# A GpSimd memset moved ahead of the first weight loads, and one W1 piece moved into an earlier group of tiled matmuls

## The chip, the cores and the metric

The kernel runs on one core of a Trainium2 chip. The metric is the device time of one execution in microseconds (us). Every execution also has a span, from the first to the last instruction in the trace; the span is about 1.8 us under the time. One core has no second die to compare with, so "fast" in the run lists means only that an execution is within 1.5% of the fastest of its kernel.

## The reference, cut to what matters

```python
def _attn_ref(x, state):              # x: (8, 8, 512, 64), state: (8, 8, 32, 64)
    a = softmax(scale * x @ state^T)
    xread = a @ state
    a2 = softmax(scale * state @ x^T)
    sread = a2 @ x
    return concatenate([xread, sread], axis=2)

def _moe_ref(x, w_in, w_out):         # w_in: (512, 2048), w_out: (2048, 512)
    h = x @ w_in
    return (h * sigmoid(h)) @ w_out
```

The attention output, 8 x 544 rows of 512, goes through the two-layer network. The kernel doesn't form `xread`. It folds the state into the weights: for each batch b it computes W(b) = state(b) @ w_in, called W0 and W1 for batches 0 and 1, and then h = a @ W(b). W has 2048 columns and is computed in pieces of up to 512.

## The kernel before

Each piece of W is eight small matmuls, placed on 64 x 32 tiles of the array:

```python
def w1_mms(b, cols, new=bank):
    ...
    for f, n in cols:
        for hg in range(2):
            pss[f, hg] = new([128, 512], FP32, "ps_w1")
        for s in range(4):
            for hg in range(2):
                ...
                nc.tensor.matmul(pss[f, hg][ds(32 * s, 32), 0:n],
                                 stT[ds(r, 64), b, h // 2, s % 2, :],
                                 w_in_sb[ds(r, 64), h // 2, ds(f, n)],
                                 ..., tile_position=(r, 32 * s))
```

The matmuls write into buffers called PSUM banks. `bank` hands out the banks a2 and a3 in turn; `new_h` hands out the two buffers h1. The first batch runs through 12 steps. `upto` issues first-layer products (g1, the matmuls called h), `G2` second-layer products (called o, or o_a for two of the row blocks):

```python
W0 = {2: (512, 512), 6: (1024, 512), 10: (1536, 512)}
W1_AT = {4: 0, 6: 512}
LEAD0 = [2, 2, 2, 2, 2, 3, 2, 1, 3, 3, 2, 3]
T3 = {1: (0, 1), 2: (2,), 3: (3,), 4: (4,), 5: (5,), 6: (6,)}
for ft in range(12):
    upto(min(ft + LEAD0[ft], ready))
    if ft == 1:
        place_one_state(1, transpose_one_state(st1_n), nc.vector)
    if ft in W0:
        pss = w1_mms(0, [W0[ft]])
        if ft in W1_AT:
            pss1 = w1_mms(1, [(W1_AT[ft], 512)], new_h)
        w1_out(0, [W0[ft]], both, pss)
        ...
    elif ft in W1_AT:
        w1_cols(1, [(W1_AT[ft], 512)], both)
    ...
    for tt in range(3):
        G2(0, tt, ft)
    for i in T3.get(ft, ()):
        G2(0, 3, i)
```

The loads at the start: x of batch 0 in two halves on the sync queue, the weights from GpSimd behind a small identity matrix. GpSimd later casts a quarter of the second half of x.

```python
make_identity(nc, ident)            # GpSimd
load_w_in(0, 128); load_w_in(128, 384)
load_w_out(0, 2); load_w_out(2, 2)
...                                 # state of batch 1
load_w_in(512); load_w_out(4, 4)
...
cast_x(0, nc.gpsimd, 0, 1, 4, 4)    # a quarter of the second half of x
...
for i in range(3):                  # at 21.6 us
    ones_beside_x(i, nc.gpsimd)     # two memsets each
```

The softmax here doesn't subtract the row's maximum and nothing guards it: scores larger than these inputs give would overflow.

## Time and profile before

| | before |
|---|---|
| median of 4 executions | 212.99 us (212.90 to 213.12) |
| the profiled execution | 214.55 us, span 212.8 |
| TensorE busy | 97% of the span |
| first second-layer matmul (o) | 13.84 us |

In the lines of the profile, PE is TensorE's matmul, PEld its weight load, DVE VectorE, ACT ScalarE, POOL GpSimd and SP the sync queue; L468 is line 468 of the kernel.

How to read it: TensorE is the bound, so a gain has to come from TensorE's list of work or from the 13 us before that list runs without holes. The profiled execution is over 1.4 us slower than each of the four timed ones.

### The profile page before, as it was taken

The page shows a single profiled execution, that of the slowest core. Times are in us where ns is not written, and L with a number is a line of the kernel's source. Part 1 is how long each engine was busy: PE and PEld are TensorE (multiplying, and loading weights), DVE is VectorE, ACT ScalarE, POOL GpSimd, SP SyncE. Part 2 cuts the span into 40 slices and gives each one's busy share as a digit, 9 for nine tenths or more (in the row PEclk, how much of TensorE's full clock was granted, in tenths as well). Part 3 has the DMA queues.
Part 4 walks back from the last instruction along what each step waited for, and adds up shares of the span by engine and source line. Part 5 has one row for each costly group of instructions (what it writes and reads, how often), then busy time and mean ns, then how long its engine had stood idle before and what let it go on. Part 6 is the DMA issues. An engine that isn't in the chain of part 4 may idle for free.

```text
span 212.8 us, 3839 instructions
## 1 busy us (share of the span) xinstructions
PE 205.8 (97%) x1550; PEld 97.9 (46%) x1575; DVE 73.8 (35%) x146; ACT 139.1 (65%) x244; POOL 39.9 (19%) x62
## 2 busy tenths in 40 slices
PE   7899999999999999999999999999999999999993
PEld 2543445345444434444444444444444444466653
DVE  2672246855851137104410752143512306100011
ACT  2685667899676877699469856886775256644410
POOL 8393213702420122012200302000200000000000
PEclk9999999999999999999999999999999999999998
DMA  5999999995639567464826429114230121011112
GB/s 189 192 205 207 285 261 313 249 242 203 99 78 265 174 130 170 101 195 102 218 64 211 79 53 240 49 52 99 65 83 17 64 82 52 0 49 49 52 49 99
DMA packets 42929, 28.65 MB, mean 135 GB/s; under 512 B 28064, under 2 KB 37792, under 8 KB 42912
## 3 DMA queue, kind: packets, MB, share of 16 engines
q1 hardware_dynamic: 36720, 20.65, 36.3%
q0 software_dynamic: 5904, 7.64, 17.4%
q8 instruction: 12, 0.20, 0.4%
q10 hardware_dynamic: 288, 0.13, 0.2%
q14 instruction: 5, 0.04, 0.1%
HBM read 17.43 MB, written 8.91 MB: 124 GB/s over the span
## 4 chain that ended last, share of the span: by engine, by line
PE 94%; DMA 2%; DVE 1%; issue 1%; ACT 0%
PE o L563 50%; PE h L522 26%; PE ps_w L468 4%; PE h L543 3%; PE o_a L563 3%; DMA x_f<-in_x_dram 2%; PE o_part L585 2%; PE ps_xt L252 1%; PE ps_sr L415 1%; PE ps_busy L165 1%; PE ps_sc L305 1%; PE ps_scT L331 1%; DVE W L159 1%; PE ps_at L397 0%; ACT xT L157 0%
## 5 line engine op out<-in xcount | busy, mean ns | idle before, releaser
L563 PE MATMUL o<-w_out_sb,g 128*128 128x512 bf16 x481 | 129.5, 379 | 1.3 <-issue 0.5
L554 ACT ACTIVATE g<-h 128x512 bf16<-128x512 f32 (+1 forms) x143 | 81.3, 573 | 35.3 <-PE h L522 20.6
L563 PEld LDWEIGHTS <-g 128*128 128x128 bf16 x528 | 50.2, 98 | 58.9 <-issue 3.8
L522 PE MATMUL h<-aT,W 128*128 128x512 bf16 x247 | 73.1, 379 | 0.2
L159 DVE COPY o_sb<-o 128x512 f32<-128x512 f32 x15 | 10.4, 690 | 91.9 <-PE o L563 87.3
L522 PEld LDWEIGHTS <-W 128*128 128x128 bf16 x254 | 24.4, 98 | 30.7 <-issue 1.2
L159 DVE CAST W<-ps_w 128x512 bf16<-128x512 f32 (+2 forms) x36 | 22.3, 658 | 23.8 <-PE ps_w L468 23.8
L157 ACT ACTIVATE W<-ps_w 128x512 bf16<-128x512 f32 (+1 forms) x32 | 16.3, 562 | 10.2 <-PE ps_w L468 10.2
L159 POOL CAST x_nat<-x_f 128x512 bf16<-128x512 f32 x24 | 14.6, 648 | 33.2 <-DMA x_f<-in_x_dram 33.2
L157 ACT ACTIVATE o_sb<-o 128x512 f32<-128x512 f32 x16 | 9.5, 597 | 14.3 <-PE o L563 11.8
L361 POOL TENSOR_TENSOR an<-e,rcn 128x512 bf16<-128x512 bf16 x5 | 7.6, 1517 | 49.1 <-DVE rcn L359 49.1
L468 PE MATMUL ps_w<-w_in_sb,stT 64*32 64x512 bf16 (+2 forms) x264 | 10.2, 374 | 0.0
L543 PE MATMUL h<-xmT,w_in_sb 128*128 128x256 bf16 x64 | 9.6, 273 | 0.1
L563 PE MATMUL o_a<-w_out_sb,g 128*128 128x512 bf16 x30 | 9.4, 379 | 0.1
L543 PEld LDWEIGHTS <-w_in_sb 128*128 128x128 bf16 x64 | 6.3, 98 | 3.9
L165 PE MATMUL ps_busy<-busy 128*128 128x512 bf16 x15 | 6.8, 563 | 1.2 <-DVE warm L172 1.2
L358 DVE TENSOR_REDUCE rs<-e 128x32 f32<-128x1024 bf16 x5 | 6.1, 1210 | 2.1 <-DMA e<-eT 2.1
L345 ACT ACTIVATE eT<-ps_scT 128x512 bf16<-128x512 f32 x10 | 5.4, 594 | 1.6 <-PE ps_scT L331 1.6
L784 ACT ACT_TABLE_LOAD x5 | 6.4, 1283 | 0.1
L381 POOL TENSOR_TENSOR an<-exp_nat,rc 128x512 bf16<-128x512 bf16 x3 | 3.1, 1046 | 17.7 <-ACT eT L345 10.8
L468 PEld LDWEIGHTS <-stT 64*32 64x32 bf16 x264 | 3.2, 90 | 5.5 <-issue 4.7
L109 POOL DMA_DIRECT2D x_f<-in_x_dram x4 | 3.3, 845 | 10.2 <-DVE x_rows L159 7.9
(76 smaller groups left out, 103.7 us busy)
## 6 DMA issues: line engine op xcount, KB each, us to landing
out_dram<-o_sb SPq DMA_DIRECT2D x33, 256.0 KB, 2.4
x_f<-in_x_dram SPq DMA_DIRECT2D x4, 1024.0 KB, 5.8
x_f<-in_x_dram POOLq DMA_DIRECT2D x2, 1024.0 KB, 11.1
w_in_sb<-in_moe_w_in_dram POOLq DMA_DIRECT2D x3, 512.0 KB, 10.1
x_f<-in_x_dram SPq DMA_DIRECT2D x2, 512.0 KB, 5.2
w_out_sb<-in_moe_w_out_dram POOLq DMA_DIRECT2D x4, 256.0 KB, 11.4
w_out_sb<-in_moe_w_out_dram POOLq DMA_DIRECT2D x2, 512.0 KB, 11.2
x_f<-in_x_dram POOLq DMA_DIRECT2D x2, 512.0 KB, 13.5
```

Source lines behind the costliest of these rows:

```text
L157: nc.scalar.activation(dst, src, func=COPY, bias=0.0)
L159: eng.tensor_copy(dst, src)
L165: nc.tensor.matmul(ps[:], busy[:, 0:128], busy[:], start=True, stop=True, skip_group_check=True)
L345: nc.scalar.activation(t[:, hg], scT_ps[hg][:], func=EXP, bias=0.0, scale=SCALE)
L358: nc.vector.tensor_reduce(rs[:], e2[b][:], axis=AX, op=ADD)
L361: eng.tensor_tensor(a[:, hg], e2[b][:, hg], rc[:, hg].to_broadcast([128, 4, 4, NS]), op=MULT)
L468: nc.tensor.matmul(pss[f, hg][ds(32 * s, 32), 0:n], stT[ds(r, 64), b, h // 2, s % 2, :], w_in_sb[ds(r, 64), h // 2, ds(f, n)], start=True, ...
L522: nc.tensor.matmul(h_ps[k][:], W1[b][:, hg, ds(128 * ft, 128)], aT[b][:, hg, :, :], start=(hg == 0), stop=(hg == 1), skip_group_check=True,)
L543: nc.tensor.matmul(ps[:, 0:256], w_in_sb[:, kt, ds(128 * ft, 128)], xmT[:, :, kt].rearrange("p t n b -> p t (n b)"), start=(kt == 0), stop ...
L554: nc.scalar.activation(g[:, 0:n], ps[:, 0:n], func=SILU, bias=0.0)
L563: nc.tensor.matmul(outs[tt][:], gt[b * NFT + ft][:, ds(128 * tt, 128)], w_out_sb[:, ft, :], start=(ft == 0), stop=(ft == NFT - 1), skip_gr ...
L784: nc.scalar.activation(warm[:], busy[:, 0:1], func=SILU, bias=0.0)
```

## The change

Its intent: GpSimd spends a memset before it starts the weight loads, so that they begin half a microsecond later and leave the DMA engines to x. And the W1 piece of step 4 joins the W0 piece of step 2, so that the tiled mode is entered once for both. The rest of the diff makes room: h products 4 and 5 take the banks of the W pieces, because the W1 piece holds both h1 buffers, and product 3 comes a step earlier.

```diff
     make_identity(nc, ident)
+    ones_beside_x(0, nc.gpsimd)
     load_w_in(0, 128)
@@ g1_half
-            pool, tag = (psA, "a1") if k == 1 else (psH, "h1")
-            h_ps[k] = pool.tile([128, 512], FP32, tag=tag, name="h1")
+            if k == 1:
+                h_ps[k] = psA.tile([128, 512], FP32, tag="a1", name="h1")
+            else:
+                h_ps[k] = (bank if k in IN_BANKS else new_h)([128, 512], FP32, "h1")
@@
+    IN_BANKS = (4, 5)
@@
-    for i in range(3):
+    for i in (1, 2):
         ones_beside_x(i, nc.gpsimd)
@@
-    W1_AT = {4: 0, 6: 512}
-    LEAD0 = [2, 2, 2, 2, 2, 3, 2, 1, 3, 3, 2, 3]
+    W1_AT = {2: 0, 6: 512}
+    LEAD0 = [2, 3, 2, 2, 2, 3, 2, 1, 3, 3, 2, 3]
@@
-        elif ft in W1_AT:
-            w1_cols(1, [(W1_AT[ft], 512)], both)
```

## The prediction

> **What bounds the kernel now.** I read the head of the page first, then the chain of waits in order of time, then the timeline of the first 24 us, the only stretch that the change touches.
>
> ```profile
> PE 205.8 (97%) x1550; PEld 97.9 (46%) x1575; DVE 73.8 (35%) x146; ACT 139.1 (65%) x244; POOL 39.9 (19%) x62
> PE 94%; DMA 2%; DVE 1%; issue 1%; ACT 0%
> ```
>
> TensorE is busy 97% of the span and holds 94% of the chain that ends last. The other 2% is one wait, at the very start:
>
> ```profile
> 0.74 4.74 DMA x_f<-in_x_dram
> 5.51 0.57 DVE x_rows L159
> 6.12 1.03 PE ps_xt L252 x8
> ...
> 16.65 0.41 PE ps_w L468 x8
> 17.07 0.69 DVE W L159
> 17.80 0.60 PE h L522 x2
> ```
>
> The first half of x (512 KB) lands at 5.48 us and everything up to the first real matmul hangs on it through casts, transposes and softmax. From 13.4 us on, TensorE issues a 512-column matmul every 0.216 us with almost no hole. So two kinds of gain are open: x landing sooner (shifts everything), or fewer microseconds of TensorE after 13.4 us. The places where it loses pace near the change are the tiled W matmuls (ps_w):
>
> ```profile
> 16.06 0.59 PE L522 MATMUL h<-aT,W 128*128 128x512 bf16 x2
> 16.58 0.41 PE L468 MATMUL ps_w<-w_in_sb,stT 64*32 64x512 bf16 x8
> 16.92 0.61 PE L563 MATMUL o<-w_out_sb,g 128*128 128x512 bf16 x2
> ...
> 19.64 0.41 PE L468 MATMUL ps_w<-w_in_sb,stT 64*32 64x512 bf16 x8
> 19.98 0.61 PE L563 MATMUL o<-w_out_sb,g 128*128 128x512 bf16 x2
> 20.42 0.59 PE L563 MATMUL o_a<-w_out_sb,g 128*128 128x512 bf16 x2
> 20.85 1.03 PE L522 MATMUL h<-aT,W 128*128 128x512 bf16 x4
> 21.71 0.59 PE L563 MATMUL o<-w_out_sb,g 128*128 128x512 bf16 x2
> 22.14 0.59 PE L563 MATMUL o_a<-w_out_sb,g 128*128 128x512 bf16 x2
> 22.67 0.63 PE L468 MATMUL ps_w<-w_in_sb,stT 64*32 64x512 bf16 x16
> 23.23 0.60 PE L563 MATMUL o<-w_out_sb,g 128*128 128x512 bf16 x2
> ```
>
> Read starts, not durations: durations include the drain of the pipeline. The two h at 16.06 occupy 2 x 0.216 and should end at 16.49; the o after the group of eight starts at 16.92, so that group costs 0.43 us. The group of sixteen: the second o_a of 22.14 ends its turn at 22.58, the next o starts at 23.23: 0.65 us. Two groups apart cost 2 x 0.435 = 0.87, two groups together 0.65. (Where fewer records than the program has matmuls stand between two starts, as after 16.92, a record is missing; the starts show the slot.)
>
> **What the Trainium skill says.** (1) "TensorEngine Tiling (Array Packing)", section Key Properties: changing the tiling mode drains TensorE. The trace agrees: 0.09 us from 16.49 to 16.58 on entry and about 0.1 us on leaving, for each group of 64*32 between 128*128 matmuls, whatever its length. (2) "DMA: Bandwidth & Descriptors", section Issuing engines are not separate DMA queues: DMAs from any engine run on the same 16 DMA engines and interleave. This is the case for delaying the weights: leave the engines to x. The trace shows little of it to gain (below). (3) Same page, section SWDGE vs HWDGE vs iDMA: for a DMA issued from GpSimd a core of it computes the descriptors, so a memset ahead of the load delays the load. The trace agrees: the GpSimd issues stand one after another at 0.71 to 0.93 us each from 1.44 to 6.56 us.
>
> **Part 1, the memset ahead of the weights.** It moves one pair of GpSimd memsets (0.33 and 0.13 us, starts 0.29 us apart from pair to pair) from 21.6 us to 1.3 us. All GpSimd issues after it move 0.3 to 0.5 us later: the pair unpipelined is 0.33 + 0.13 = 0.46 us.
>
> ```profile
> 1.44 1.68 POOL L150 DMA_DIRECT2D w_in_sb<-in_moe_w_in_dram  x2
> 3.10 1.42 POOL L153 DMA_DIRECT2D w_out_sb<-in_moe_w_out_dram  x2
> 5.02 0.79 POOL L150 DMA_DIRECT2D w_in_sb<-in_moe_w_in_dram  x1
> 7.00 0.40 POOL L159 CAST x_rows<-x_f 128x256 bf16<-128x256 f32 x1 [0.44 <-DMA x_f<-in_x_dram]
> ```
>
> Gain: does x land sooner? In the packet records by queue, x has its queue to itself until 4.96 us; the first weight packet starts there, just when the DMA engines finish their shares of x one by one (4.99 to 5.08 on six, 5.6 to 5.95 on nine, 6.44 on the last). The half that the chain waits for has its last packet done at 4.96. The second half takes 1.42 us on most engines and the first half about the same (32 packets of 46 ns are 1.47), so the weights don't slow it either. Expected gain: 0. Whether the weights then start later at all is open: they were issued at 1.44 and started 3.5 us later, apparently behind x, so half a microsecond of later issue may be hidden.
>
> Cost: landing times from each issue against the first use (issue start + landing): w_in columns 0 to 127 land at 1.44 + 6.0 = 7.4, used 10.32; the next 384 at 2.2 + 7.5 = 9.7, used 11.25; w_out 0, 1 at 3.1 + 8.0 = 11.1, used 13.84; w_in 512 to 1023 at 5.02 + 10.1 = 15.1, used 16.58. The least room is 1.5 us, over the 0.5 lost. The GpSimd cast at 7.00 waited for x until 6.97; GpSimd comes free at 6.56 + 0.46 = 7.02 instead, so it slips by under 0.1 us, and its transposes start at 8.29, behind a warm-up matmul. Cost: 0. The later loads (from 11.42) start behind a softmax product on GpSimd and are not moved by it.
>
> **Part 2, the W1 piece.** Removed: the lone group of eight at 19.64. Added: the same eight behind the eight of 16.58. Matmuls and copies stay the same in number; one entry and one exit of the tiled mode go. On TensorE: 0.87 - 0.65 = 0.22 us. The starts give slightly more: from 16.49 to 20.85 there are sixteen matmuls of 0.216 (3.45 us) and two groups, so 0.91 for the groups with the slow first matmuls behind them; from 22.58 to 24.10 there are four (0.86) and one double group, 0.66. 0.91 - 0.66 = **0.25 us**, all on the path.
>
> Moved: the first-layer product k=3 comes one step earlier (LEAD0 2 to 3), since the W1 group takes both h1 buffers in step 2; k=4 and 5 go to the banks of the W group. I count the new order from 14.49: four h (0.86), the state transpose at 15.35, five second-layer matmuls to 16.49, sixteen tiled ones to 17.14, four to 18.00, then k=4. Its waits: the W0 copies, DVE 17.05 to 17.74 and ACT 17.18 to 17.77, are done before 18.00 (before, k=4 came at 17.80, right on the DVE copy); the W1 copies follow to 18.4 on DVE and 18.3 on ACT, and ACT is then free for the silu of k=4 (18.6). The h1 buffers are wanted again by k=6 at 20.6, long free. The W1 group needs the state of batch 1:
>
> ```profile
> 15.18 0.96 DVE L159 COPY stT<-ps_st 64x64 bf16<-64x64 bf16 x4 [1.18 <-PE ps_st L206]
> ```
>
> Its transpose moves 0.43 us back, behind the h of k=3, so these copies end at 16.14 + 0.43 = 16.57, and the second group's matmuls are due at about 16.81, with weight loads of 0.09 before them. It fits with 0.1 to 0.2 us over: the tightest place of the change. Later stages move 0.25 us forward as one piece: w_in 1024 lands at 11.42 + 8.8 = 20.2 for a use at 22.4, w_in 1536 at 25.4 for a use at 27.6, x of batch 1 at 28.3 for its second cast at about 29.3.
>
> **The sum.** 212.99 - 0 - 0.25 = 212.74, rounded to 212.7 us.
>
> **Rivals.** (a) *x lands sooner.* For it: all loads share engines, and nine of them begin x 0.7 us later than the first six, for a reason that I don't see. If GpSimd's descriptor work at 1.4 to 2.3 us has a part in that, the delay brings some of it to the front: 0.2 to 0.5 us more, 212.2 to 212.5. Against it: no weight packet moves before 4.96. (b) *The state copies come too late.* TensorE would stand in the double group for 0.1 to 0.3 us and eat the gain: 212.8 to 213.0. Against it: the count above, though by little. (c) *Weights become the wait.* If the delay grew in the queue to over 1 us, w_in 512 would arrive after its use at 16.5 and push everything: 213.2 or more. Against it: the room of 1.5 us, and an unbroken stream of packets that a later issue doesn't interrupt. (d) *The gain is given back* at a later wait for DMA (x of batch 1) or DVE: 213.0. Against it: TensorE has the chain from 13 us to the end.
>
> **Range and chances.** The three runs before spread 0.22 us, so the median itself is good to about 0.1. With (a) below and (b), (c), (d) above, 212.3 to 213.0. Two per cent is 4.3 us; nothing here reaches that. Faster 0.01, same 0.98, slower 0.01.
>
> **What would show it.** Part 1: the first weight load issued near 1.9 us, x still landing at 5.5 (half a microsecond sooner would prove rival (a)), no wait for a weight. Part 2: sixteen ps_w in one piece near 16.6, none near 19.6, the o after them 0.65 us after the last matmul before them, k=4 at about 18.0 with no wait, and k=6 at 20.6 instead of 20.85. From there all starts should be 0.25 us earlier to the end. Wrong if PE waits for DVE stT in the double group, if W copies hold k=4, or if the shift is lost by 52 us.

## The result

The changed kernel took 212.86 us (median of 4, 212.69 to 213.12) against 212.99 us. The ratio is 0.9995, with a 95% interval from 0.9977 to 1.0012: the same within 2%, as predicted, and too small to be seen in so few executions. (A ratio is the mean time of one kernel's fast runs over that of the other's of the same rounds, so not quite the ratio of the medians quoted.)

The page of the changed kernel, the two lines that answer to those shown of before:

```profile
PE 205.3 (97%) x1575; PEld 96.8 (46%) x1575; DVE 74.0 (35%) x146; ACT 139.2 (66%) x244; POOL 39.5 (19%) x62
PE 95%; DMA 2%; DVE 1%; ACT 0%; issue 0%; DVEq 0%
```

Nothing has moved in the bound. The span, though, is 210.9 us against 212.8, which is 1.9 us, where the timed executions differ by 0.13 us. Its chain of waits (start, duration, what) begins:

```profile
0.74 4.17 DMA x_f<-in_x_dram
5.01 0.44 DVE x_rows L159
```

x landed at 4.91 us instead of 5.48, which at first looks like rival (a) of the prediction. The timeline of TensorE shows a second difference. These are the same eight transposes of x, before and then changed:

```profile
6.12 1.03 PE L252 MATMUL ps_xt<-ident,x_rows 128*128 128x128 bf16 x8 [0.44 <-DVE x_rows L159]
```

```profile
5.50 0.62 PE L253 MATMUL ps_xt<-ident,x_rows 128*128 128x128 bf16 x8 [0.54 <-DVE x_rows L159]
```

1.03 us against 0.62 for equal work: TensorE was still slow in the trace of before. Warm-up matmuls (on zeros, to keep TensorE busy) stand 0.43 us apart in both traces until 3.7 us, and 0.22 us apart from 4.4 us on in the changed one. The clock records of the traces say when full speed was granted: at 10.2 us in the trace of before, at 3.9 us in the changed one. The Trainium skill, "TensorE: Matmul & The Clock Gate", section Part 1: The HAM clock gate, says that the window which watches activity runs free, so the number of slow matmuls at the start varies from run to run. The traces here agree: the same kernel before was at full speed from 10.2 us in its first trace, and from 6.9 and 5.1 us in e1 and e12 below. The two late ones of the 14 (10.2 us, and 10.6 in e4) are also the two in which the first half of x landed last, at 5.48 and 5.34 us; in the other twelve it landed at 4.79 to 5.11 us, and full speed came at 3.9 to 6.9 us. So the 1.9 us is no effect of the change, and the stage of the tiled matmuls must be read by itself.

The timeline of TensorE, changed kernel (start, duration, engine, line, operation):

```profile
13.80 0.59 PE L566 MATMUL o<-w_out_sb,g 128*128 128x512 bf16 x2
14.23 0.81 PE L566 MATMUL o_a<-w_out_sb,g 128*128 128x512 bf16 x3
14.99 0.64 PE L469 MATMUL ps_w<-w_in_sb,stT 64*32 64x512 bf16 x16
15.56 0.60 PE L566 MATMUL o<-w_out_sb,g 128*128 128x512 bf16 x2
...
19.03 1.03 PE L525 MATMUL h<-aT,W 128*128 128x512 bf16 x4
...
20.85 0.63 PE L469 MATMUL ps_w<-w_in_sb,stT 64*32 64x512 bf16 x16
```

The sixteen stand together and no group stands near 18. GpSimd's timeline has the surprise of part 1:

```profile
1.25 0.31 POOL L115 MEMSET x_rows<- 128x256 bf16 x1
...
1.50 0.11 POOL L118 MEMSET x_rows<- 128x16 bf16 x1
1.55 1.68 POOL L150 DMA_DIRECT2D w_in_sb<-in_moe_w_in_dram  x2
```

The first load is issued at 1.55 us, and before at 1.44. The memset delays the weights by 0.11 us, not by half a microsecond. Its pair takes 0.36 us, from 1.25 to 1.61 us. Of that, 0.06 us run beside the last step of the identity matrix (which ends at 1.31), 0.13 us fill the gap that stood ahead of the load before, and 0.06 us run beside the load; 0.11 us are left.

### The profile page after: what moved, and what is told of

Its sections match the earlier page's. It is cut to its first block, busy times and chain, and to the rows that moved or that the text cites. A ratio compares the mean times of both kernels' runs of the same rounds, so it can differ in the third digit from the quotient of the medians.

```text
span 210.9 us, 3866 instructions
## 1 busy us (share of the span) xinstructions
PE 205.3 (97%) x1575; PEld 96.8 (46%) x1575; DVE 74.0 (35%) x146; ACT 139.2 (66%) x244; POOL 39.5 (19%) x62
## 4 chain that ended last, share of the span: by engine, by line
PE 95%; DMA 2%; DVE 1%; ACT 0%; issue 0%; DVEq 0%
PE o L566 51%; PE h L525 26%; PE ps_w L469 4%; PE h L546 3%; PE o_a L566 3%; DMA x_f<-in_x_dram 2%; PE o_part L588 2%; PE ps_sr L416 1%; PE ps_xt L253 1%; PE ps_sc L306 1%; PE ps_scT L332 1%; PE ps_busy L165 1%; PE ps_at L398 0%; PE h L507 0%; DVE W L159 0%; ACT xT L157 0%
## 5 line engine op out<-in xcount | busy, mean ns | idle before, releaser
L566 PE MATMUL o<-w_out_sb,g 128*128 128x512 bf16 x496 | 131.8, 379 | 0.0
L525 PE MATMUL h<-aT,W 128*128 128x512 bf16 x254 | 74.5, 379 | 0.1
L566 PE MATMUL o_a<-w_out_sb,g 128*128 128x512 bf16 x32 | 10.0, 379 | 0.0
L165 PE MATMUL ps_busy<-busy 128*128 128x512 bf16 x16 | 5.8, 481 | 1.2 <-DVE warm L172 1.2
## 6 DMA issues: line engine op xcount, KB each, us to landing
w_in_sb<-in_moe_w_in_dram POOLq DMA_DIRECT2D x3, 512.0 KB, 10.2
```

The lines of the kernel that those rows point to most:

```text
L165: nc.tensor.matmul(ps[:], busy[:, 0:128], busy[:], start=True, stop=True, skip_group_check=True)
L525: nc.tensor.matmul(h_ps[k][:], W1[b][:, hg, ds(128 * ft, 128)], aT[b][:, hg, :, :], start=(hg == 0), stop=(hg == 1), skip_group_check=True,)
L566: nc.tensor.matmul(outs[tt][:], gt[b * NFT + ft][:, ds(128 * tt, 128)], w_out_sb[:, ft, :], start=(ft == 0), stop=(ft == NFT - 1), skip_gr ...
```

## The experiments

My theory: the gain is one entry and exit of the tiled mode, some 0.2 us; the memset does nothing; the rest is the start of the single execution. Rivals: the memset improves the order of x and weights; the weights become the wait; the gain is given back later. Twelve kernels ran, five rounds or more each; 29 executions of the kernel before stood beside them (mean 213.00 us, standard deviation 0.14).

**e1_null and e12_null_again: the kernel before, unchanged.** No edit.

> The kernel before, unchanged: ratio 1.000, and the width of its interval is what the later ratios must beat. Its profile should show whether the start in the first profile of before (first h matmul at 12.64 us, span 212.8) is typical: if the timed median of 212.99 us means a span near 211.2 (span is 1.8 us under the time in both profiled runs), a typical execution starts its first h near 11.1 us. Rival: this start is typical for before, and the memset removed 1.6 us of it.

> The kernel before again, unchanged: ratio 1.000. Its trace is a third one of the start without the memset: w_in 128 to 511 expected at 9.6 to 10.3 us, and x of the first half at 4.9 us or, with a late start of the DMA engines, 5.5.

Measured: e1 213.17 us median, ratio 1.0006 (0.9994 to 1.0018); e12 212.83 us, 0.9997 (0.9983 to 1.0010). So single ratios are good to some 0.12%, or 0.25 us, which is the size of the whole effect: it has to be read from traces and from pooled runs. Their spans are 211.3 and 211.1 us, and x landed at 4.88 and 4.86 us. The early start is typical of the kernel before too, and the rival that the memset removed 1.6 us has fallen. e12's w_in 128 to 511 came at 9.45 us, earlier than I had expected for a trace without the memset.

The timeline of TensorE in e12 is a fair picture of the kernel before:

```profile
14.34 0.59 PE L522 MATMUL h<-aT,W 128*128 128x512 bf16 x2
14.86 0.41 PE L468 MATMUL ps_w<-w_in_sb,stT 64*32 64x512 bf16 x8
15.21 0.61 PE L563 MATMUL o<-w_out_sb,g 128*128 128x512 bf16 x2
...
17.92 0.41 PE L468 MATMUL ps_w<-w_in_sb,stT 64*32 64x512 bf16 x8
...
20.95 0.63 PE L468 MATMUL ps_w<-w_in_sb,stT 64*32 64x512 bf16 x16
```

From the first group (14.86) to the group of step 6 (20.95) it takes 6.09 us; in the changed kernel above 20.85 - 14.99 = 5.86, and 5.88 in e2 and e9.

**e2_after and e9_after_again: the whole change.** No edit to the changed kernel.

> The whole change again, with more rounds. Theory (one entry and one exit of the tiled mode saved, nothing from the memset): 0.25 us faster, ratio 0.9988. Rival (the gain is given back later): ratio 1.000. In the trace: from the first h matmul to the end 0.25 us shorter than in the trace of e1.

> The whole change a third time, beside e10 to e12 on one chip, to settle the memset's share. If the memset does nothing: the same as e10 within 0.1 us in the runs after the profiled one, about 0.22 us under before. If it brings the weights in earlier: w_in columns 128 to 511 landing at 9.3 to 9.65 us (seen with it in five of six traces) and e10 slower by 0.1 to 0.3 us.

Measured: 212.78 us, ratio 0.9990 (0.9977 to 1.0003), and 212.75 us, 0.9989 (0.9976 to 1.0001). All 14 executions of the changed kernel (with the four of the result) have a mean of 212.81 us, 0.19 us under the 29 of before; from the two spreads I estimate this as good to about 0.1 us. The expectation of e2 measured from the first h matmul. That doesn't serve, since waits stand among the first h: from the first one on record to the first o it takes 0.84 us in e2 and e12 and 1.2 us in e1 and e9, with the change and without it. So I measure from the first o (table below), a change of yardstick after the expectation.

**e3_w1_only and e10_w1_again: the W1 piece moves, the memset doesn't.**

```diff
-    ones_beside_x(0, nc.gpsimd)       # ahead of the weights
...
-    for i in (1, 2):
+    for i in range(3):
```

> Only the W1 piece moves; the memset stays at 21 us. Theory: all of the gain, 0.25 us, ratio 0.9988, the same as e2. Rival (the memset brings x or the weights into better order): less than half of e2's gain.

> Only the W1 piece again. Memset does nothing: 0.2 us under before, as e9. Memset matters: w_in 128 to 511 landing at 9.6 to 10.3 us (seen without it in all four traces), waits of TensorE for w_in or w_out as in the profile of e3, and a time 0.1 to 0.3 us over e9.

Measured: 212.91 us, ratio 0.9997 (0.9985 to 1.0009), and 212.92 us, 0.9998 (0.9985 to 1.0010). By the expectations of e9 and e10 this speaks for the memset: e10 is 0.17 us over e9, its four executions after the profiled one (212.92 to 213.28) all lie over those of e9 (212.72 to 212.75), and w_in 128 to 511 landed at 9.67 us. Against it, e3 and e2 in their call overlap, and the trace of e10 has no such wait for a weight and the full gain after the first o (table below). The trace of e3 does not; its timeline of TensorE has a wait that no other has at this length:

```profile
17.99 0.59 PE L524 MATMUL h<-aT,W 128*128 128x512 bf16 x2
18.88 0.59 PE L565 MATMUL o<-w_out_sb,g 128*128 128x512 bf16 x2 [0.29 <-DMA w_out_sb<-in_moe_w_out_dram]
```

The two h at 17.99 take 0.43 us of issue, so this o was due at 18.42 and came 0.46 us late, for w_out 4 to 7. The group of step 2 had been 0.11 us late, too, for w_in 512. In the record of landings, fifteen DMA engines were done with that load by 17.61 us and the last at 18.84. At 16.33 us a packet of 16 KB on the instruction queue had begun, which took 0.98 us. The Trainium skill, "Runtime: NRT & Kernel Launch", section Instruction fetch mechanics, says that engines refill their instructions in blocks of 16 KiB through a DMA queue; each trace has such a packet of 0.9 to 1.0 us at 16.0 to 17.8 us. The records don't name the engine of a packet, so that this packet held up that load is an inference.

**e4_memset_only and e11_memset_again: the memset moves, the W1 piece doesn't.**

```diff
     make_identity(nc, ident)
+    ones_beside_x(0, nc.gpsimd)
...
-    for i in range(3):
+    for i in (1, 2):
```

> Only the memset moves ahead of the weights. Theory: ratio 1.000 within the interval of e1, first weight packet 0.1 us later at most, x landing as in e1. Rival (x lands sooner): 0.2 to 0.5 us faster, with the first half of x landing that much sooner than in e1. Rival (weights become the wait): slower by 0.1 to 0.5 us with TensorE waiting for w_in on the chain.

> Only the memset again. In the profile of e4 TensorE warmed up late and the execution took 214.7 us, so its trace says little. Memset does nothing: the time of before within 0.1 us. Memset delays the GpSimd cast of x (6.62 us in e2 against 6.51 in e3): 0.1 us slower than before in executions with an early warm-up. Memset brings weights in earlier: 0.1 us faster, since before has 0.3 us of room for w_in 512 anyway.

Measured: 213.14 us, ratio 1.0019 (0.9997 to 1.0040), and 213.00 us, 1.0000 (0.9987 to 1.0013). e4's mean contains its profiled execution of 214.70 us, which has x at 5.34 us and a late warm-up as in the first trace of before; without it the other five average 213.16. So by itself the memset gains nothing that these runs can see. In all twelve experiments the first weight packet started between 4.90 and 5.17 us.

The table reads each trace in two parts. "After the first o" is the span minus the start of the first second-layer matmul, so the start of the execution is out of it.

| trace | first o, us | after the first o, us | w_in 512 to 1023 landed / used, us |
|---|---|---|---|
| before (first trace) | 13.84 | 198.91 | 15.13 / 16.58 |
| e1, before | 12.44 | 198.90 | 14.86 / 15.18 |
| e12, before | 12.12 | 198.94 | 14.75 / 14.86 |
| e4, memset only | 14.01 | 198.91 | 14.79 / 16.75 |
| e11, memset only | 12.28 | 198.91 | 14.82 / 15.02 |
| changed (first trace) | 12.23 | 198.69 | 14.95 / 14.99 |
| e2, changed | 12.24 | 198.72 | 14.81 / 14.98 |
| e9, changed | 12.44 | 198.70 | 14.56 / 15.18 |
| e10, W1 only | 12.32 | 198.70 | 14.96 / 15.06 |
| e3, W1 only | 12.41 | 199.25 | 15.22 / 15.26 |

Five traces without the W1 move lie within 0.04 us of each other, at a mean of 198.91; four with it lie within 0.03, at 198.70. The move of the W1 piece is worth 0.21 us of TensorE, with or without the memset, unless a weight is late.

The last column shows what the first trace hid. In an execution with an early start w_in 512 lands 0.1 to 0.6 us before its use, not 1.5 us. A difference of 0.04 us is no room at all: it is what e3, e5 and e8 show, where TensorE stood for this load, and the first trace of the changed kernel shows it too (its group began 0.02 us late).

**e5_split: the reverse dose.** The kernel before, with the double group of step 6 taken apart.

```diff
-    W1_AT = {4: 0, 6: 512}
+    W1_AT = {4: 0, 8: 512}
```

> The reverse dose: the kernel before with its one double group of W matmuls (step 6) taken apart, the W1 piece in a group of its own in step 8. Theory (each lone group of eight costs one entry and one exit of the tiled mode): 0.2 to 0.25 us slower than before, ratio 1.0010 to 1.0012, all of it between the first second-layer matmul and the end. Rival (the order of buffers, not the groups, made the gain): no change.

Measured: 213.41 us, ratio 1.0022 (1.0008 to 1.0035): slower, and clear of the noise. From the o after the group of step 2 to the end its trace takes 212.11 - 16.03 = 196.08 us; e1 and e12 take 195.83 and 195.85. So the third lone group costs 0.24 us. This run leaves the order of the h products and their buffers alone, so the gain isn't owed to those parts of the diff. The other 0.2 us of the timed difference isn't explained by the edit. In its profile w_in 128 to 511 landed at 10.33 us and TensorE waited 0.94 us of its warm-up stretch for it, and w_in 512 came at 15.64 us, 0.12 us too late. So the timed difference alone would not prove the price of a group; the stretch of the trace behind that wait does.

**e6_late: the weights issued 1 us later.**

```diff
     make_identity(nc, ident)
+    ones_beside_x(0, nc.gpsimd)
+    late = pers.tile([128, 1024], BF16)
+    nc.gpsimd.memset(late[:], 0.0)
...
-    for i in range(3):
+    for i in (1, 2):
```

> The kernel before with the memset pair and a further memset of 1024 columns ahead of the weights, so the first weight load is issued about 1 us later than before (2.4 to 2.7 us instead of 1.44). Theory (the weights stand behind x, so a later issue is hidden): first weight packet still at 4.9 to 5.1 us, w_in 512 landing at 14.8 to 15.2 as before, time as before, ratio 1.000. Rival (the weights follow the issue): first packet near 6 us, w_in 512 landing near 16 us and TensorE waiting for it: 0.5 to 1 us slower.

Measured: 213.78 us (213.76 to 213.83), ratio 1.0037 (1.0024 to 1.0050), 0.8 us slower. The transfers did what the theory said: first weight packet at 5.10 us, w_in 512 at 14.74. The time did not. GpSimd's timeline, then that of the weight loads of TensorE:

```profile
2.44 1.69 POOL L150 DMA_DIRECT2D w_in_sb<-in_moe_w_in_dram  x2
...
7.50 0.47 POOL L159 CAST x_rows<-x_f 128x256 bf16<-128x256 f32 x1
```

```profile
8.02 0.45 PEld L255 LDWEIGHTS <-x_rows 128*128 128x128 bf16 x8 [0.43 <-POOL x_rows L159]
```

In GpSimd's list the cast of x stands behind all weight loads, and the last of them was issued at 6.77 us here. So the cast came at 7.50 us instead of 6.5 to 6.6, and the transposes of the second half of x wait for it: they start at 8.03 us, against 7.01 to 7.39 in the executions of e1, e2, e3 and e12. They start 0.64 us behind those of e1, whose full clock came as late as here (6.8 and 6.9 us), and the span is 0.64 us longer too. After the first o the trace takes 198.91 us, as before. My expectation asked only about the DMA queue and forgot the engine that feeds it.

**e7_fill: a hole of TensorE filled.** All the traces above have a hole of 0.22 us in step 10, where h waits for the DVE copy of W. One o moves there.

```diff
-    T3 = {1: (0, 1), 2: (2,), 3: (3,), 4: (4,), 5: (5,), 6: (6,)}
+    T3 = {1: (0, 1), 2: (2,), 3: (3,), 4: (4,), 5: (5,), 6: (6,), 10: (7,)}
...
-    G2(0, 3, 7)
     scores(1, 0, new=new_h)
```

> The changed kernel with one second-layer matmul (row block 3, step 7) moved into step 10, where TensorE stands 0.22 us for the DVE copy of W at 27.26 in all traces. Theory: this hole closes and nothing opens later: 0.2 us faster than the changed kernel, 0.4 to 0.45 faster than before, ratio 0.998. Rival: the scores of batch 1, which lose the matmul ahead of them, wait instead: ratio as for the changed kernel, 0.999.

Measured: 212.89 us (212.85 to 212.94), ratio 0.9995 (0.9983 to 1.0008): not faster than the changed kernel. The hole closed, but two opened, where the transposes of the softmax of batch 1 now wait for their inputs. The weight loads in its trace:

```profile
34.72 0.23 PEld L398 LDWEIGHTS <-an 128*128 128x128 bf16 x4 [0.40 <-POOL an L382]
...
35.27 0.23 PEld L398 LDWEIGHTS <-an 128*128 128x128 bf16 x4 [0.27 <-DVE an L382]
```

They cost the matmul pace 0.08 and 0.10 us, which is most of the 0.22; from the o behind the group of step 6 to the end the trace takes 189.51 us, against 189.52 to 189.54 in the three of the changed kernel. The gain was given back, one stage after the one that I had named as the rival. In this trace step 4 also stood 0.15 us, and the wait ended at 18.33 us, just behind the landing of w_out 4 to 7 at 18.29.

**e8_fill_wout: w_out 4 to 7 in two halves.**

```diff
-    load_w_out(4, 4)
+    load_w_out(4, 2)
...
+    load_w_out(6, 2)
     load_w_in(1024)
```

> As e7, and the load of w_out 4 to 7 taken in two halves in the same order of the queue, the second issued with the later loads. Theory: w_out 4 and 5 land near 16.2 us instead of 17.4 to 18.8, so that the use at 18.2 can no longer wait as it did in the profile of e3 (0.25 us); mean time 0 to 0.1 us under e7 and no more stragglers. Rival: the second half comes later than its use at step 6 and makes a wait: slower than e7.

Measured: 213.16 us (212.66 to 213.32), ratio 1.0005 (0.9992 to 1.0017). w_out 4 and 5 landed at 16.62 us and step 4 had no wait, nor had step 6 for the second half. (The expectation gives e3's wait as 0.25 us; by the pace of TensorE it was 0.46.) But w_in 128 to 511 came at 10.06 us and w_in 512 at 15.37 us, 0.11 us too late, in a part of the kernel that is the same as in e7, where they came at 9.28 and 14.58. Why they came late in this trace I can't say, and the other four executions have none. No version beat the changed kernel.

## Why the prediction was right or wrong, point by point

**The time, 212.7 us against 212.86, and 0.25 us of gain against 0.21.** Right, but the time by itself says little: "no change", 212.99 us, lay inside the range of 212.3 to 213.0 as well, and the four executions couldn't tell the two apart. The mechanism is shown by the traces: the gain is in four with the W1 move, in none of the five without it, and a group taken apart costs 0.24 us (e5).

**The size of part 2.** The term that was over-sized is the double group, read from step 6: 0.65 us to the next o, or "one double group, 0.66" with the slower first matmuls behind it. In step 2 these are 0.68 to 0.69 and 0.70 us, and 0.91 - 0.70 is the 0.21 measured. What the prediction missed is the bank of the second matmul of the group. By the code it is the one that the transposed state of batch 1 was in, and the four copies of that state are just leaving it. In e9 (the copies, then the group):

```profile
14.21 0.96 DVE L159 COPY stT<-ps_st 64x64 bf16<-64x64 bf16 x4 [1.60 <-PE ps_st L207]
15.18 0.67 PE L469 MATMUL ps_w<-w_in_sb,stT 64*32 64x512 bf16 x16
```

The copies end at 15.17 us and the second matmul starts at 15.22, 0.042 us after the first, where such neighbours otherwise stand 0.003 apart. It starts 0.055 us behind the end of the copies in five traces alike (changed, e2, e7, e9 and e10). In e3 and e8 the whole group came 0.11 us late for its weights, when the copies had been done for 0.13 us; its second matmul follows 0.003 us behind the first, and without those 0.11 us the group costs 0.65 us, as predicted. In e3:

```profile
15.26 0.63 PE L468 MATMUL ps_w<-w_in_sb,stT 64*32 64x512 bf16 x16
```

So rival (b) came true by 0.04 us. The prediction had the copies ready in time for the second half of the group, which needs the data; it was the first half that waited. That it waits for the bank is read from the code and these times; no run gave it another bank.

**"All GpSimd issues after it move 0.3 to 0.5 us later."** Wrong: 0.11 us. I added up durations of memsets that overlap each other and the instruction ahead of them, and I did not ask whether the 0.13 us ahead of the load was free. ("0.71 to 0.93 us each" also leaves out the load of the state, after which the next issue came 0.53 us later.)

**"Expected gain: 0" of part 1.** Right for the memset alone (e11, 1.0000). e6 shows that the start of the weights doesn't follow their issue: a load issued 1 us later started at the same time. That it is x which holds them isn't shown. For it: in every trace the first weight packets start as the packets of x in flight become fewer. Against it: in the first trace of before only 6 to 12 packets of x and the state were in flight from 2.2 to 2.9 us, fewer than the 16 engines, and no weight moved then either. Beside the W1 move, the pooled executions leave a question open: 14 of the changed kernel have a median of 212.77 us (mean 212.81) and 10 with the W1 piece alone 212.92 (mean 212.96), so in the times the W1 piece alone shows hardly any of the gain. w_in 128 to 511 landed at 9.26 to 10.06 us in seven traces with the memset and at 9.45 to 10.33 in six without (means 9.54 and 9.79). The ranges overlap, and the executions of one kernel differ by as much. Whether the memset protects the weights of the changed kernel stays open.

**"The least room is 1.5 us" for the weights.** Wrong, and it is the most important miss. The number came from an execution whose first o was 1.4 to 1.7 us later than in e1 and e12, with weights on time. With an early start the room of w_in 512 is 0.6 us at most, and it was used up in e3, e5, e8 and the first trace of the changed kernel. Even in its own trace the least room was 1.4 us: w_in 128 to 511 was issued at 2.36 us, not 2.2, and landed at 9.83, not 9.7. And the list leaves out w_out 4 to 7, for which e3 and e7 waited. Rival (c), which I put aside with this room, may be why a gain of 0.21 us shows less surely in the times than in the traces: moving TensorE's work forward brings it closer to loads that do not move. With one trace for each run, that isn't shown.

**"Cost: 0" for the GpSimd cast.** Nearly right for this change and shown fragile by e6: the cast starts at 6.62 us in e2 and 6.51 in e3, and in both TensorE's weight loads wait 0.2 us for it, but its matmuls only some 0.05 us.

**"Later stages move 0.25 us forward as one piece."** Right, but for the size: from the o behind the group of step 6 to the end, every trace takes between 189.49 and 189.56 us, but for e5, which has a group left to do. The whole gain lies between the first o and that one, 9.39 us in the traces of before and 9.17 to 9.18 in those of the change. In e7 a later wait did take back a further gain.

## What to carry to other kernels

Before reading any slack from a trace, compare the time of the profiled execution with the timed ones: a trace of a slow start shows loads with room that they don't have. Each group of tiled matmuls between full ones cost the same 0.2 us here, whether it held eight or sixteen, so put groups side by side, but count the buffers and the loads that the earlier group needs. Work put ahead of a DMA issue also delays everything else that its engine has to do, and that can cost more than the transfer.

## What the Trainium skill lacked or had wrong

- "TensorEngine Tiling (Array Packing)", section Key Properties, says that a mode change drains TensorE, without a size. Here a lone group of eight matmuls on 64 x 32 tiles between full ones took 0.43 us of issue and a group of sixteen 0.65: about 0.2 us for each entry with its exit.
- "DMA: Bandwidth & Descriptors", section Queues, rings and completion order, says that a DMA engine takes turns between the queues that have work. Here weights issued at 1.43 us and at 2.44 us both sent their first packet only at 4.9 to 5.1 us. In every trace the number of packets of x in flight last reached 16 at 4.95 to 5.19 us, and the first weight packet started at 4.90 to 5.17. No turns were taken before that; the records don't say why.
- "Runtime: NRT & Kernel Launch", section Instruction fetch mechanics, has the 16 KiB refill, but not its cost to others: such a packet took 0.9 to 1.0 us at 16 to 18 us in these traces, and the load in flight then ended on its last DMA engine up to 1.2 us after the others (17.61 and 18.84 in e3). Leaving out e8, whose load is another, the last engine was 0.55 to 1.23 us behind in seven of the eight traces in which the packet began by 16.33 us, and 0.02 to 0.53 us in the five in which it began at 16.6 or later. The link is inferred.
- No page gives the delay of a DMA issue by small memsets ahead of it on GpSimd: 0.11 us here, for memsets of 0.31 and 0.11 us.
